# Attention and two mixtures of experts: a low part on GpSimd, an earlier gather, a reordered end

## The chip, the cores and the metric

The kernel runs on one core of a Trainium2 chip. The metric is device time in microseconds (us) of one execution, as the median of several. Before the change it is 914.06 us, the median of three runs (911.19 to 917.10). Each of the core's engines has its own instruction queue and runs it in order: TensorE (PE; PEld is its loading of weights), VectorE (DVE), ScalarE (ACT), GpSimd (POOL) and SyncE (SP), which here only issues DMAs.

## What is computed

Causal attention without a projection, then two mixtures of experts of which each token takes one expert. Cut to what matters (4 batches, 12 heads, 448 positions, 64 per head; 1792 tokens of 768, 8 experts, 1024 hidden):

```python
scores = scale * q @ k.T                  # masked above the diagonal
attn = exp(scores - max) / (sum + 1e-9)
x = attn @ v                              # heads side by side: 1792 x 768
# layer one: expert = argmax(normalized x . normalized embedding / tau)
# layer two: expert = argmax(x @ w_gate + modality_bias[modality_id])
for e in range(8):
    mask = expert_idx == e
    h = maximum(x[mask] @ w1[e], 0)
    out[mask] = gate_w[mask] * (h @ w2[e])
```

## The kernel before

Products that need more than one pass of precision are made from a high and a low half of each factor: `ah`, `al` are the halves of the attention weights `ex`, `w2h`, `w2l` those of a weight matrix, `hh`, `hl` those of the hidden layer, `xh`, `xl` those of the tokens.

**Attention** goes over 24 pairs of heads (two heads `e` = 0, 1 at a time). One loop, with `g` from 0 to 26, holds four stages of four different pairs: scores and exponentials of pair `g`, turned and split weights of pair `t = g - 1`, products with the values of pair `v = g - 2`, and a piece of the routing of layer one for pair `r = g - 3`. The code order is the order of every engine's queue. The weights of pair `g` leave the exponential as `ex`. `halves_hi` (L428), at the end of iteration `g`, makes `ah` (f16) of head 0 on ScalarE (L432) and of head 1 on GpSimd (L434), and has SyncE turn each with a transposing DMA (L425) into `th`. `halves_lo` (L436), one iteration later, makes `al = ex * ASC - ah` of both heads on VectorE (L439), and SyncE turns each into `tl`. In between VectorE makes `pl` (L455), the low part of those blocks that TensorE turns itself (L449). Two iterations after its exponentials, `values` (L484) multiplies `th`, `tl`, `ph`, `pl` with the halves of the values, and `combine` (L495 to L503) scales the result with `rinv` into `xb`.

On SyncE an iteration issues the loads for a later pair (L375, L381), the two `tl` of pair `g - 1`, at most times a store of finished tokens (L533), and the two `th` of pair `g`. On GpSimd it scales the queries of a later pair (L385), makes `ah` of head 1, and splits values (L163).

The routing of layer one is a generator; `tick()` takes a step of it after certain instructions on VectorE, so that its small steps stand between those of attention. When a batch of 448 tokens has its experts, GpSimd scatters its rows of `meta` (L653), a table of which token goes to which place.

**Each layer of experts** runs in blocks of 128 tokens. `gather_early` (L765 to L743) takes a block's rows of `meta` into `mg` and its tokens into `xg`; the first one stands in iteration 24 (`g == NPR`). TensorE turns them (L957) and multiplies (L975 to L977: `w1h xh`, `w1l xh`, `w1h xl`). The second layer has no routing inside, and works with up to `MAXB` = 21 blocks; here 17 are run, sections `j` up to 16. Section `j` computes the hidden layer of block `j` and the `down` product of block `j - 1` (L1040). `h_split` makes `hh` and `hl`, `x_squares` turns the tokens of block `j + 2` on VectorE into `xr` (L948). `split_w(2, ...)` makes the eight parts of `w2h` (ACT, L707) and `w2l` (VectorE, L709) of an expert from `w2r`, which was loaded long before. After the last section the last block's product runs in `down_last` (L1057), in two halves of 384 columns; if the expert changes at the last block (`cl > 0`, as here), `split_w(2)` stands ahead of it. Each half is scaled (L1070) into `yb` or `yT` and scattered to the output by GpSimd (L1071).

Of the kernel before, what the change touches and what calls it, by code (L numbers as in the profile page):

```python
# [35 lines left out]
ALIGN = 1  # L36
SPREAD = 4
# [19 lines left out]
def attention_two_moe_kernel(  # L57
# [370 lines left out]
    def halves_hi(g):  # L428
        for e in range(2):
            ah, ex = ahs[g % NAH][:, e, :, :CP], exs[g % NEX][:, e, :ND]  # L430
            if e == 0:
                act.activation(ah, ex, AF.Copy, scale=ASC)  # L432
            else:
                pool.tensor_scalar(out=ah, in0=ex, scalar1=ASC, scalar2=1.0, op0=ALU.mult, op1=ALU.mult)  # L434
            transposed(ths[g % NTH], ahs[g % NAH], e)

    def halves_lo(g, es):
        for e in es:
            vec.scalar_tensor_tensor(out=als[g % NAH][:, e, :, :CP], in0=exs[g % NEX][:, e, :ND], scalar=ASC,  # L439
                                     in1=ahs[g % NAH][:, e, :, :CP], op0=ALU.mult, op1=ALU.subtract)  # L440
            transposed(tls[g % NTH], als[g % NAH], e)
            tick()
# [351 lines left out]
    for g in range(NPR + 3):  # L794
# [28 lines left out]
        if 0 <= t < NPR:  # L823
            halves_lo(t, (0,))
        next(parts[0], None)
        if 0 <= t < NPR:
            halves_lo(t, (1,))
# [55 lines left out]
        if g + 1 < NPR:  # L883
            split_v(g + 1)
        if LEAD <= g <= NPR:
            for c in range(g - LEAD, KD if g == NPR else g - LEAD + 1):
                load_lead(m1, 1, c)
# [8 lines left out]
        if g == NPR:  # L896
# [5 lines left out]
            m1.gather_early((0,), 2 * S)  # L902
# [154 lines left out]
    def down_last(m, mg):  # L1057

        ops = ps_a.tile([P, 2, 512], F32, tag="av", name="o")
# [4 lines left out]
        for n in range(2):  # L1064
            cols = slice(n * 384, (n + 1) * 384)
            for f in range(KF):
                for w, h, st in ((w2h, hh, 0), (w2l, hh, 1), (w2h, hl, 2)):
                    pe.matmul(ops[:, n, :384], lhsT=h[f // KH][:, f % KH], rhs=w[f][:, cols],
                              start=(f == 0 and st == 0), stop=(f == KF - 1 and st == 2))
            act.activation(yhs[n], ops[:, n, :384], AF.Copy, scale=mg[:, 2:3])  # L1070
# [232 lines left out]
    def switches(m, tab):  # L1303
# [17 lines left out]
        vec.tensor_mul(chg, chg, actv[0:1])  # L1321
        vec.tensor_reduce(out=chg[:, 0:1], in_=chg[:, :MAXB], axis=AX.X, op=ALU.add)
# [17 lines left out]
    def run(m, is_full):  # L1340
# [8 lines left out]

        def section(j):  # L1350
# [10 lines left out]
            near = m.routed and j >= NBLK - 1  # L1361
            if 1 < j and j + 2 < MAXB:
                m.gather_q(j + 2)
            if near and j < NBLK:
                early_x(j)
# [4 lines left out]
            if FIRSTQ <= j + 1 < MAXB:  # L1370
                prep(m, j + 1, ra, MAXB if near and j >= NBLK else FIRSTQ + 1)
            if near and j >= NBLK:
# [28 lines left out]
            elif j > 1:  # L1401
                down(m, m.mg(j - 1), h_split)
# [30 lines left out]
        if not follow:  # L1433
            with tc.If(cl > 0) as other:  # L1434
                split_w(2)
# [102 lines left out]
```

## Time and profile before

| | |
|---|---|
| median of three runs | 914.06 us (911.19 to 917.10) |
| the profiled run | 911.23 us |
| its span in the trace | 909.4 us (1.8 us lie around it) |
| TensorE busy | 854.2 us (94%) |
| loading of weights | 738.0 us (81%) |
| VectorE busy | 681.7 us (75%) |
| ScalarE, GpSimd busy | 421.7 us (46%), 411.2 us (45%) |

The profile comes from one execution. A busy share is a mean over stretches with different limits, so each stretch has to be read by itself. A timeline row gives the start, the duration, engine, line, operation and what it writes and reads; a bracket at its end is the time for which the engine stood idle before, and what ended that. The rows of SyncE (SPq) are the time in which it issues a DMA; the DMA lands later.

### The profile page before, as it was taken

To read this page: it belongs to the slowest core of one execution; us is meant where nothing else is said; L and a number is where in the kernel's file an instruction comes from. 1 tells how busy PE (TensorE), PEld (TensorE's weight loads), DVE (VectorE), ACT (ScalarE), POOL (GpSimd) and SP (SyncE) were. 2 spreads that over 40 slices of the span, in tenths; PEclk is the share of its full clock that TensorE was granted. 3 is DMA by queue.
4 is the path that set the end of the run, shared out by engine and by line. 5 is a ranking of instruction groups with operands and counts; after the bars stand their busy time and mean duration, and the time that the engine had idled before them with its cause. 6 is when DMAs were issued, how large, how long until landed. Compare 5 with 4: busy or idle time off the path is not lost. (4 is left out here: it accounts for less than half of the span.)

```text
span 909.4 us, 20926 instructions
## 1 busy us (share of the span) xinstructions
PE 854.2 (94%) x6914; PEld 738.0 (81%) x6914; DVE 681.7 (75%) x1810; ACT 421.7 (46%) x777; POOL 411.2 (45%) x457
## 2 busy tenths in 40 slices
PE   5899999998598899999999999999999999999994
PEld 2577877777476799998898999988899898898984
DVE  5698999998694766788846874468886678976793
ACT  3576867776345564566524742254112133312323
POOL 4243345353345355454434564441653544544531
PEclk9899999999899999999999999999999999999998
DMA  6478776898617775588515563120281223511110
GB/s 200 104 144 149 174 158 149 173 161 184 223 28 241 270 289 188 189 278 300 206 38 176 188 227 121 39 90 6 58 332 39 66 86 134 186 48 54 54 38 16
DMA packets 92950, 131.94 MB, mean 145 GB/s; under 512 B 56877, under 2 KB 61283, under 8 KB 92784
## 3 DMA queue, kind: packets, MB, share of 16 engines
q1 hardware_dynamic: 79872, 103.25, 39.7%
q0 software_dynamic: 12912, 26.83, 9.5%
q8 instruction: 60, 0.98, 0.5%
q14 instruction: 106, 0.87, 0.3%
HBM read 101.48 MB, written 19.92 MB: 133 GB/s over the span
## 5 line engine op out<-in xcount | busy, mean ns | idle before, releaser
L759 POOL DMA_INDIRECT xg<-x,xi x128 | 137.2, 1072 | 102.4 <-DMA x<-yb,mg 55.0
L975 PE MATMUL h<-w1h,xh 128*128 128x512 f32 x408 | 164.2, 403 | 1.0 <-ACT xh L959 1.0
L976 PE MATMUL h<-w1l,xh 128*128 128x512 f32 x408 | 161.1, 395 | 0.8 <-DVE w1l L709 0.8
L977 PE MATMUL h<-w1h,xl 128*128 128x512 f32 x408 | 160.7, 394 | 0.0
L1040 PE MATMUL o<-w2h,hh 128*128 128x384 f32 x528 | 137.6, 341 | 0.2 <-ACT hh L989 0.2
L1040 PE MATMUL o<-w2h,hl 128*128 128x384 f32 x528 | 135.3, 337 | 0.9 <-DVE hl L990 0.9
L1040 PE MATMUL o<-w2l,hh 128*128 128x384 f32 x528 | 134.6, 336 | 0.0
L1017 DVE STREAM_TRANSPOSE hs<-h 32x256 f32<-32x256 f32 x240 | 107.1, 446 | 14.5 <-PE h L977 8.5
L422 ACT ACTIVATE ex<-sc,nm 112x112 f32<-112x112 f32 (+1 forms) x192 | 85.4, 496 | 48.8 <-DVE nm L417 47.9
L1040 PEld LDWEIGHTS o<-w2h,hl 128*128 128x128 f32 x528 | 95.3, 188 | 1.3 <-DVE hl L990 1.3
L1040 PEld LDWEIGHTS o<-w2l,hh 128*128 128x128 f32 x528 | 95.2, 188 | 0.4 <-DVE w2l L709 0.3
L1040 PEld LDWEIGHTS o<-w2h,hh 128*128 128x128 f32 x528 | 94.0, 188 | 1.8 <-ACT hh L989 0.4
L976 PEld LDWEIGHTS h<-w1l,xh 128*128 128x128 f32 x408 | 77.1, 189 | 18.2 <-DVE w1l L709 3.2
L1023 ACT ACTIVATE hh<-hs 128x512 fp32r<-128x512 f32 x30 | 18.4, 630 | 158.2 <-DVE hs L1017 79.6
L977 PEld LDWEIGHTS h<-w1h,xl 128*128 128x128 f32 x408 | 76.9, 189 | 17.7 <-DVE xl L960 0.3
L975 PEld LDWEIGHTS h<-w1h,xh 128*128 128x128 f32 x408 | 77.1, 189 | 16.6 <-ACT xh L959 1.1
L709 DVE TENSOR_TENSOR w1l<-w1r,w1h 128x1024 fp32r<-128x1024 f32 x66 | 76.4, 1220 | 9.2 <-ACT w1h L707 8.4
L417 DVE TENSOR_REDUCE nm<-sc 112x1 f32<-112x112 f32 (+1 forms) x192 | 74.6, 438 | 6.0 <-PE sc L411 5.9
L709 DVE TENSOR_TENSOR w2l<-w2r,w2h 128x768 fp32r<-128x768 f32 x78 | 68.7, 952 | 7.4 <-ACT w2h L707 6.6
L707 ACT CAST w1h<-w1r 128x1024 fp32r<-128x1024 f32 x64 | 62.4, 1047 | 9.3 <-PE h L977 5.2
L411 PE MATMUL sc<-r 64*112 64x112 f32 (+3 forms) x384 | 62.4, 447 | 3.9 <-DVE rt_ren L175 3.9
L948 DVE STREAM_TRANSPOSE xr<-xg 128x768 f32<-128x768 f32 x31 | 50.4, 1626 | 19.2 <-DMA xg<-x,xi 14.4
(327 smaller groups left out, 1776.9 us busy)
## 6 DMA issues: line engine op xcount, KB each, us to landing
w1r<-in_w1a SPq DMA_DIRECT2D x48, 512.0 KB, 6.2
w2r<-in_w2a SPq DMA_DIRECT2D x64, 384.0 KB, 6.4
r<-in_kqP SPq DMA_DIRECT2D x24, 448.0 KB, 4.5
w1r<-in_w1b SPq DMA_DIRECT2D x18, 512.0 KB, 5.7
w2r<-in_w2b SPq DMA_DIRECT2D x24, 384.0 KB, 6.5
vr<-in_vh SPq DMA_DIRECT2D x24, 224.0 KB, 4.3
x<-xb SPq DMA_DIRECT2D x16, 336.0 KB, 3.8
xg<-x,xi POOLq DMA_INDIRECT x128
```

The lines of the kernel that those rows point to most:

```text
L411: pe.matmul(scs[2 * g + e, c][:CP, :n], lhsT=r[rs, 1, c * CP : n], rhs=r[rs, 0, :n], start=False, stop=True, skip_group_check=True)
L417: vec.tensor_reduce(out=nms[h][:, c : c + 1], in_=scs[h, c][:CP, : CP * (c + 1)], axis=AX.X, op=ALU.min)
L422: act.activation(dst, scs.pop((h, c))[:CP, :n], AF.Exp, bias=nms[h][:, c : c + 1], scale=-1.0)
L707: act.copy(hi[k], r[k])
L709: vec.tensor_sub(lo[k], r[k], hi[k].bitcast(F32))
L759: pool.indirect_dma_start(out=xgs[j % 3][:, q * (D // Q) : (q + 1) * (D // Q)], out_offset=None, in_=quarters, in_offset=IND(ap=xi[:, q : ...
L948: vec.transpose(xr.rearrange("p k (q r) -> p q k r", q=Q), xgs[j % 3].rearrange("p (q r k) -> p q k r", q=Q, k=KD))
L975: pe.matmul(hps, lhsT=xh[:, c], rhs=w1h[c][:, ns], start=(c == 0), stop=False)
L976: pe.matmul(hps, lhsT=xh[:, c], rhs=w1l[c][:, ns], start=False, stop=False)
L977: pe.matmul(hps, lhsT=xl[:, c], rhs=w1h[c][:, ns], start=False, stop=(c == KD - 1))
L1017: vec.transpose(hr[cols, :, rows], hps[rows, q * 256 : (q + 1) * 256].rearrange("p (c k) -> p k c", c=QR))
L1040: pe.matmul(ops[:, n, :384], lhsT=h[f // KH][:, f % KH], rhs=w[f][:, n * 384 : (n + 1) * 384], start=(f == 0 and st == 0), stop=(f == KF - ...
```

## The change

Three edits.

*Attention.* The low part of head 1 moves from VectorE to GpSimd. GpSimd now scales `ex` of head 1 in place, copies it to `ah` and subtracts; this stands in `halves_hi`, at the end of iteration `g`. `halves_lo` keeps head 0 alone, with one `tick()` instead of two.

*First gather of layer one.* `gather_early((0,), ...)` stands at the end of iteration 22 instead of 24.

*End of layer two.* In sections from `j = 13` on, three parts of `w2` (`SOON`) are split ahead of `h_split` when this block is the last and its expert differs (`split_last`, a load and a branch on ACT and VectorE), and `x_squares` moves behind that. Ahead of `down_last` only five parts are left. `down_last` puts its halves into two PSUM tiles, and each half is scaled by ACT and VectorE together, 192 columns each.

```diff
--- before.py
+++ after.py
@@ -34,6 +34,7 @@
 ASC = 32768.0
 TICKS = 6
 ALIGN = 1
+SOON = 3
 SPREAD = 4
 LATE = 12
 LEAD = 18
@@ -431,15 +432,17 @@
             if e == 0:
                 act.activation(ah, ex, AF.Copy, scale=ASC)
             else:
-                pool.tensor_scalar(out=ah, in0=ex, scalar1=ASC, scalar2=1.0, op0=ALU.mult, op1=ALU.mult)
+                pool.tensor_scalar(out=ex, in0=ex, scalar1=ASC, scalar2=1.0, op0=ALU.mult, op1=ALU.mult)
+                pool.tensor_scalar(out=ah, in0=ex, scalar1=1.0, scalar2=1.0, op0=ALU.mult, op1=ALU.mult)
             transposed(ths[g % NTH], ahs[g % NAH], e)
-
-    def halves_lo(g, es):
-        for e in es:
-            vec.scalar_tensor_tensor(out=als[g % NAH][:, e, :, :CP], in0=exs[g % NEX][:, e, :ND], scalar=ASC,
-                                     in1=ahs[g % NAH][:, e, :, :CP], op0=ALU.mult, op1=ALU.subtract)
-            transposed(tls[g % NTH], als[g % NAH], e)
-            tick()
+        pool.tensor_tensor(out=als[g % NAH][:, 1, :, :CP], in0=ex, in1=ah, op=ALU.subtract)
+        transposed(tls[g % NTH], als[g % NAH], 1)
+
+    def halves_lo(g):
+        vec.scalar_tensor_tensor(out=als[g % NAH][:, 0, :, :CP], in0=exs[g % NEX][:, 0, :ND], scalar=ASC,
+                                 in1=ahs[g % NAH][:, 0, :, :CP], op0=ALU.mult, op1=ALU.subtract)
+        transposed(tls[g % NTH], als[g % NAH], 0)
+        tick()
 
     def turned_part(g, part):
 
@@ -821,10 +824,8 @@
         if g < NPR:
             both(expo, g, 1, ticks=False)
         if 0 <= t < NPR:
-            halves_lo(t, (0,))
+            halves_lo(t)
         next(parts[0], None)
-        if 0 <= t < NPR:
-            halves_lo(t, (1,))
         if g == NPR + 2:
             warm(ps_T, "T", WV)
         if 0 <= r < NPR:
@@ -882,6 +883,8 @@
             split_v(0)
         if g + 1 < NPR:
             split_v(g + 1)
+        if g == NPR - 2:
+            m1.gather_early((0,), 2 * S)
         if LEAD <= g <= NPR:
             for c in range(g - LEAD, KD if g == NPR else g - LEAD + 1):
                 load_lead(m1, 1, c)
@@ -899,7 +902,6 @@
             wb = left("wb", 1)
             w1l = [wb.tile([P, F], F32R, name=f"w1l{c}") for c in range(KD)]
             w2r = [wb.tile([P, D], F32, name=f"w2r{f}") for f in range(KF)]
-            m1.gather_early((0,), 2 * S)
             load_lead(m1, 2)
         if g == NPR + 2:
             split_w(1, (), range(3, KD))
@@ -1056,7 +1058,7 @@
 
     def down_last(m, mg):
 
-        ops = ps_a.tile([P, 2, 512], F32, tag="av", name="o")
+        ops = (o_tile()[:, 0], ps_h.tile([P, 512], F32, tag="h", name="o1"))
         yhs = yb[:, :384], yT.rearrange("p k c -> p (k c)")[:, :384]
         for n in range(2):
             vec.tensor_scalar(out=two[n], in0=mg[:, 1:2].bitcast(I32), scalar1=2.0, scalar2=float(n), op0=ALU.mult,
@@ -1065,9 +1067,10 @@
             cols = slice(n * 384, (n + 1) * 384)
             for f in range(KF):
                 for w, h, st in ((w2h, hh, 0), (w2l, hh, 1), (w2h, hl, 2)):
-                    pe.matmul(ops[:, n, :384], lhsT=h[f // KH][:, f % KH], rhs=w[f][:, cols],
+                    pe.matmul(ops[n][:, :384], lhsT=h[f // KH][:, f % KH], rhs=w[f][:, cols],
                               start=(f == 0 and st == 0), stop=(f == KF - 1 and st == 2))
-            act.activation(yhs[n], ops[:, n, :384], AF.Copy, scale=mg[:, 2:3])
+            act.activation(yhs[n][:, :192], ops[n][:, :192], AF.Copy, scale=mg[:, 2:3])
+            vec.tensor_scalar_mul(yhs[n][:, 192:], ops[n][:, 192:384], mg[:, 2:3])
             i = pool.indirect_dma_start(out=out.rearrange("n (k d) -> (n k) d", k=2), out_offset=IND(ap=two[n], axis=0),
                                         in_=yhs[n], in_offset=None, bounds_check=2 * NT - 1, oob_is_err=False)
             apart(i.ins, "out")
@@ -1319,6 +1322,8 @@
         if m.routed:
             vec.tensor_tensor(out=tab[:, 1, 1:], in0=chg[:, 1:], in1=actv[0:1, :MAXB], op=ALU.add)
         vec.tensor_mul(chg, chg, actv[0:1])
+        if not m.routed:
+            vec.tensor_copy(tab[:, 1, 1:], chg[:, 1:])
         vec.tensor_reduce(out=chg[:, 0:1], in_=chg[:, :MAXB], axis=AX.X, op=ALU.add)
         vec.tensor_copy(tab[:, 1, 0:1], chg[:, 0:1])
 
@@ -1347,6 +1352,10 @@
             with tc.If(ends < j + 2):
                 follow.gather_early((0, 1), what="x")
 
+        def split_last(j):
+            with tc.If(nc.values_load(tab[0:1, 1, j : j + 1], engines=[ENG.Activation, ENG.DVE], min_val=0, max_val=1) > 0):
+                split_w(2, range(SOON), range(SOON))
+
         def section(j):
 
             late = j >= LATE
@@ -1358,18 +1367,19 @@
                 split_next(m, j - 1, 2, tab)
             begin = m.routed and j != 2
             finish = m.routed and j not in (1, 3)
-            near = m.routed and j >= NBLK - 1
+            near = j >= NBLK - 1
+            ahead = MAXB if m.routed and j >= NBLK else FIRSTQ + 1
             if 1 < j and j + 2 < MAXB:
                 m.gather_q(j + 2)
-            if near and j < NBLK:
+            if m.routed and j == NBLK - 1:
                 early_x(j)
             if j + 4 < MAXB:
                 m.gather_m(j + 4)
                 m.gather_r(j + 4)
             ra, rb = (route_a(), chain(route_g(), route_b())) if finish else (iter(()), iter(()))
             if FIRSTQ <= j + 1 < MAXB:
-                prep(m, j + 1, ra, MAXB if near and j >= NBLK else FIRSTQ + 1)
-            if near and j >= NBLK:
+                prep(m, j + 1, ra, ahead)
+            if m.routed and j >= NBLK:
                 early_x(j)
             h0 = up(j, 0)
             if begin:
@@ -1399,7 +1409,9 @@
             if j > 1 and m.routed:
                 down(m, m.mg(j - 1), h_turned, {4: h_turn})
             elif j > 1:
-                down(m, m.mg(j - 1), h_split)
+                down(m, m.mg(j - 1), lambda: (split_last(j) if near else None, h_split()))
+                if near and j + 2 < MAXB:
+                    x_squares(j + 2)
             else:
                 if m.routed:
                     h_turn()
@@ -1432,7 +1444,7 @@
                 section(j)
         if not follow:
             with tc.If(cl > 0) as other:
-                split_w(2)
+                split_w(2, range(SOON, KF), range(SOON, KF))
                 down_last(m, gt)
             with other.Else():
                 down_last(m, gt)
```

How this moves instructions, in three places. First SyncE's queue in the middle of attention; `r` and `vr` are the loads for later pairs, `x` is the store of tokens, `x2` means both heads. Before:

```order
L375 DMA r_2442<-in_kqP 128x896
L381 DMA vr_2444<-in_vh 112x512
L425 DMA_TRANSPOSE tl_226<-al_220 128x4x112 x2
L533 DMA x_62<-xb_484 112x768
L425 DMA_TRANSPOSE th_221<-ah_217 128x4x112 x2
L375 DMA r_2643<-in_kqP 128x896
```

And of the change:

```order
L376 DMA r_2456<-in_kqP 128x896
L382 DMA vr_2458<-in_vh 112x512
L426 DMA_TRANSPOSE tl_226<-al_220 128x4x112
L536 DMA x_62<-xb_488 112x768
L426 DMA_TRANSPOSE th_221<-ah_217 128x4x112 x2
L426 DMA_TRANSPOSE tl_224<-al_219 128x4x112
L376 DMA r_2658<-in_kqP 128x896
```

The second transpose of the `tl` has moved from behind the loads to behind the two `th` of its own pair; the first `tl` of a pair follows behind the next loads, and so after it.

Second GpSimd's queue in iterations 22 and 23; `r...<-vr` and the row below it split values, `ld_full` is a flag that says whether the block is full. Before, iteration 23 into what follows it:

```order
L163 TENSOR_TENSOR r_242<-vr_4133 112x8x64
L163 TENSOR_TENSOR r_4783<-r_242 112x512
L434 TENSOR_SCALAR ah_218<-ex_216 112x4x112
L160 TENSOR_SCALAR w1h_5027<-w1r_329 128x1024
L160 TENSOR_SCALAR w1h_5028<-w1r_330 128x1024
L652 MEMSET pad 128x1
L653 DMA meta_63<-mt_138,r1sir_5115 14336x8
```

...and after four such scatters the gathers, with the root of the last batch's routing behind them:

```order
L653 DMA meta_63<-mt_138,r1sir_5115 14336x8
L765 TENSOR_LOAD ld_fullm_199
L765 ISA x2
L767 COMPARE_AND_BRANCH
L740 DMA mg_323<-meta_63,ld_idxm_197 128x8
...
L743 DMA xg_322<-x_62,mg_323 128x768
...
L170 TENSOR_TENSOR rt_sr_5422<-r1ss_5273,half 112x4
```

And of the change:

```order
L438 TENSOR_TENSOR al_219<-ex_215,ah_217 112x4x112
L164 TENSOR_TENSOR r_242<-vr_4140 112x8x64
L164 TENSOR_TENSOR r_4808<-r_242 112x512
L768 TENSOR_LOAD ld_fullm_199
...
L743 DMA mg_323<-meta_63,ld_idxm_197 128x8
...
L746 DMA xg_322<-x_62,mg_323 128x768
...
L435 TENSOR_SCALAR ex_216<-ex_216 112x448
L436 TENSOR_SCALAR ah_218<-ex_216 112x4x112
L438 TENSOR_TENSOR al_220<-ex_216,ah_218 112x4x112
L161 TENSOR_SCALAR w1h_5052<-w1r_329 128x1024
```

The gathers have moved from behind the third batch's scatters to ahead of the three instructions that make head 1's halves of the last pair; those three are one before.

Third VectorE's queue at the end of section 16 of layer two, the last that runs here; `hs` are the turned hidden values, `gt` a copy of the block's rows of `meta`. Before:

```order
L1017 STREAM_TRANSPOSE hs<-h 32x8x32 x8
L948 STREAM_TRANSPOSE xr<-xg_322 128x4x6x32
L1024 SCALAR_TENSOR_TENSOR hl_5490<-hs,hh_5492 128x512
L1024 SCALAR_TENSOR_TENSOR hl_5491<-hs,hh_5493 128x512
L1410 COPY gt<-mg_327 128x8
L1422 COMPARE_AND_BRANCH
```

And of the change:

```order
L1019 STREAM_TRANSPOSE hs<-h 32x8x32 x8
L1356 TENSOR_LOAD t_tabm_317
L1356 COMPARE_AND_BRANCH
L712 TENSOR_TENSOR w2l_5519<-w2r_5230,w2h_5521 128x768
L712 TENSOR_TENSOR w2l_5520<-w2r_5231,w2h_5522 128x768
L712 TENSOR_TENSOR w2l_5489<-w2r_5232,w2h_5523 128x768
L1356 UNCONDITIONAL_BRANCH x2
L1026 SCALAR_TENSOR_TENSOR hl_5514<-hs,hh_5516 128x512
L1026 SCALAR_TENSOR_TENSOR hl_5515<-hs,hh_5517 128x512
L950 STREAM_TRANSPOSE xr<-xg_322 128x4x6x32
L1422 COPY gt<-mg_327 128x8
L1434 COMPARE_AND_BRANCH
```

Three parts of `w2l` and a branch stand ahead of `hl`, and `xr` has moved from ahead of `hl` to behind it.

## Rows read from the trace of the kernel before

**Rows 1.** Windows of two pairs: length, busy us (count) per engine, TensorE's clock, DMA

```profile
99.06:107.14 8.08, 8.08 (x145) 6.43 (x145) 7.43 (x21) 6.43 (x15) 3.15 (x5) 1.00 0.88 198
126.35:136.11 9.76, 8.75 (x148) 6.74 (x148) 9.70 (x32) 5.70 (x13) 3.14 (x4) 1.00 0.63 132
```

**Rows 2.** Waits of TensorE, 40 to 232 us: total us, times, longest

```profile
PE av L484 <- DMA tl<-al: 2.9, 6, 0.7
PE tb L449 <- DVE pl L455: 2.6, 5, 0.8
PE tb L512 <- DVE xb L503: 1.5, 3, 0.6
```

**Rows 3.** Timeline of one smooth pair, GpSimd, VectorE and TensorE: start, duration, what

```profile
104.30 0.56 POOL L434 TENSOR_SCALAR ah<-ex 112x448 f16<-112x448 f32 x1 [4.85 <-ACT ex L422]
...
106.95 0.56 POOL L385 TENSOR_SCALAR r<-r 128x448 f32<-128x448 f32 x1
...
105.70 0.17 DVE L495 TENSOR_SCALAR rinv<-av 112x8 f32<-112x8 f32 x1 [0.39 <-PE tb L488]
...
107.83 0.61 DVE L439 SCALAR_TENSOR_TENSOR al<-ex,ah 112x448 f16<-112x448 f32 x1
108.37 0.61 DVE L455 SCALAR_TENSOR_TENSOR pl<-tb,ph 112x448 f16<-112x448 f32 x1
108.90 0.61 DVE L439 SCALAR_TENSOR_TENSOR al<-ex,ah 112x448 f16<-112x448 f32 x1
...
109.04 0.30 PE L449 MATMUL tb<-ident,ex 112*112 112x112 f32 x1
```

**Rows 4.** Groups of VectorE and GpSimd, 40 to 232 us: busy us, mean ns, idle before

```profile
L439 DVE SCALAR_TENSOR_TENSOR al<-ex,ah 112x448 f16<-112x448 f32 x44 | 27.5, 625 | 0.0
...
L163 POOL TENSOR_TENSOR r<-r 112x512 bf16<-112x512 f32 x21 | 21.8, 1040 | 1.6
```

**Rows 5.** Timeline: VectorE beside GpSimd's subtractions, at the first pair and in routing

```profile
19.16 1.04 POOL L163 TENSOR_TENSOR r<-vr 112x512 f32<-112x512 f32 x1
...
19.91 0.76 DVE L439 SCALAR_TENSOR_TENSOR al<-ex,ah 112x448 f16<-112x448 f32 x1
...
182.75 1.03 DVE L606 SCALAR_TENSOR_TENSOR r1lgr<-r1lgr,tau_r,r1nrr 112x32 f32<-112x32 f32 x1
```

**Rows 6.** Tile tl: time to landing; timeline of SyncE and TensorE for one pair

```profile
DMA to landing us min/median/max: 3.1/4.4/5.8
...
110.84 2.50 SPq L425 DMA_TRANSPOSE tl<-al  x2
...
115.98 0.19 PE L484 MATMUL av<-vr,tl 112*128 112x64 bf16 x1
...
117.27 0.20 PE L484 MATMUL av<-vr,tl 112*128 112x64 bf16 x1 [0.65 <-DMA tl<-al]
```

**Rows 7.** Timeline of GpSimd, VectorE and TensorE where layer one begins

```profile
230.91 1.06 POOL L653 DMA_INDIRECT meta<-mt,r1sir  x1 [10.52 <-DVE ld_rowm L286]
...
241.02 1.66 POOL L740 DMA_INDIRECT mg<-meta,ld_idxm  x1 [4.93 <-DMA meta<-mt,r1sir]
...
247.33 0.17 DVE L175 TENSOR_SCALAR rt_rr<-rt_sr 112x4 f32<-112x4 f32 x1 [3.25 <-POOL rt_sr L170]
...
249.21 1.54 PE L957 MATMUL xt<-ident,xg 128*128 128x128 f32 x6 [6.51 <-DMA xg<-x,mg]
...
251.77 0.63 PE L977 MATMUL h<-w1h,xl 128*128 128x512 f32 x1
```

**Rows 8.** Timeline of VectorE, TensorE and ScalarE at the end of layer two

```profile
883.53 1.62 DVE L948 STREAM_TRANSPOSE xr<-xg 128x768 f32<-128x768 f32 x1
...
888.41 7.04 DVE L709 TENSOR_TENSOR w2l<-w2r,w2h 128x768 fp32r<-128x768 f32 x8 [1.57 <-ACT w2h L707]
...
896.84 0.44 PE L1068 MATMUL o<-w2h,hh 128*128 128x384 f32 x1 [0.72 <-ACT yb L1070]
...
901.35 0.58 ACT L1070 ACTIVATE yT<-o,gt 128x384 f32<-128x384 f32 x1 [4.56 <-PE o L1068]
```

## The prediction

> **What bounds the kernel now.** I read the windows first, then who waits for whom at TensorE, then each place that the change touches as a timeline. Attention runs to about 240 us, the first mixture of experts to about 600 us, the second to 909 us. The change touches attention and the two ends of the mixtures.
>
> In attention the windows [rows 1] show two kinds of head pair. In a smooth one (99.06 to 107.14) TensorE is busy throughout and VectorE for 7.43 of 8.08 us. In a crowded one (126.35 to 136.11), into which the routing of a finished batch is woven, VectorE is busy for 9.70 of 9.76 us and TensorE for 8.75: there VectorE sets the pace. What TensorE waited for over all pairs is short [rows 2]: 2.9 us for the transposed low part `tl`, 2.6 us for `pl`, 1.5 us for `xb`. By these waits part one can win 7.0 us at most.
>
> A busy TensorE does not mean that VectorE has room. Follow one smooth pair [rows 3]: VectorE starts `rinv` at 105.70 after waiting 0.39 us for TensorE, and `pl` ends 3.28 us later, at 108.98, with `al` of head 0 (107.83) just ahead of it. TensorE's next transposes (L449) start at 109.04, 0.06 us after `pl`. So the loop goes from `rinv` to `pl` on VectorE and from there back to the next `rinv` on TensorE, and has no slack. `al` of head 0 lies in that loop. `al` of head 1, which the change takes away, starts at 108.90, behind `pl`, in the part where VectorE later waits for TensorE.
>
> **Part one: the low part of head 1 moves to GpSimd.** VectorE loses one `al` per pair, 625 ns busy [rows 4], of which 0.53 us is pitch (108.37 to 108.90 in rows 3). GpSimd gains a scaling in place of 112x448 (a scaling, L385, takes 0.56 us [rows 3]) and a subtraction: its 112x512 subtraction takes 1040 ns [rows 4], so 448/512 of that is 0.91 us. Together 1.5 us per pair. GpSimd idled 4.85 us ahead of its `ah` [rows 3], so it has the time.
>
> The Trainium skill ("GPSIMD Engine Reference", 4.1 Engine selection) advises against this: it gives elementwise work to VectorE and calls GpSimd about 2 times slower with two inputs. By that factor the subtraction would take 1.25 us and still fit into the idle time; the rows here give 0.91 against 0.625, a factor near 1.5.
>
> What it saves: in smooth pairs nothing, since the removed `al` is not in the loop. In the crowded ones up to 0.53 us each: TensorE's eight waits for `pl` and `xb` total 4.1 us [rows 2], and eight times 0.53 is as much. I take half, **-2.0 us** (0 to -4.1), as many of those waits begin ahead of the removed instruction.
>
> What it costs on VectorE: GpSimd's later work slides by 1.5 us. In a smooth pair it now ends at 107.51 (106.95 + 0.56), just ahead of head 0's `al` at 107.83 [rows 3]; afterwards it runs to about 109.0 and covers that `al`. How far that hurts is seen at the first pair, where `al` ran under GpSimd's subtractions: 0.76 us [rows 5] instead of 0.61. So 0.15 us per pair, in the loop; with some 20 pairs and part of it absorbed I take **+2.0 us** (0 to +3). A worse row exists: L606 on VectorE, only 112x32, took 1.03 us [rows 5], the length of the GpSimd subtraction that it ran beside. That is a rival below.
>
> The Trainium skill ("GPSIMD Engine Reference", 1. Specifications) says that GpSimd shares its SBUF interfaces with VectorE and contends with instructions there that have two SBUF inputs; `al` is one, and the 0.76 us agrees. It gives no price.
>
> What it does to SyncE's queue: two transposing DMAs hold SyncE for 2.50 us [rows 6], so 1.25 us each. Now both `tl` go out behind the loads of an iteration. Afterwards `tl` of head 1 goes out directly behind the two `th`, some 2.5 us earlier, and `tl` of head 0 stays behind the loads and goes out 1.25 us later. Landing takes 3.1 to 5.8 us, median 4.4 [rows 6]. In the pair whose two went out from 110.84 TensorE first used `tl` (head 0) at 115.98, then waited 0.65 us for head 1 until 117.27 [rows 6]. Head 0 had 115.98 - 110.84 - 4.4 = 0.74 us of room; 1.25 us later it is half a microsecond late. So the six waits for head 1 (2.9 us) go, and shorter ones for head 0 come in more pairs. A wait in one pair gives a later one its time back, so I count 0.2 us in each of 20 pairs, 4 us. Net **+1.0 us** (-2.9, no pair late, to +9.5, half of 1.25 us in every pair).
>
> Part one together: +1.0 us, between -7.0 and +9.6 without the rival's hold on VectorE.
>
> **Part two: the first gather moves from pair 24 to pair 22.** TensorE waited 6.51 us for `xg`, until 249.21 [rows 7]. GpSimd's queue was the cause: the gather of `mg` stood at 241.02, after 4.93 us for the last `meta`; the gather of `xg` had to wait for it, and `rt_sr`, the root of the last batch's routing, stood behind both. Afterwards `xg` has landed some 20 us ahead of its use. On GpSimd the two gathers then stand ahead of pair 23's `ah` and hold it for some 5 us (two issues and a landing); TensorE is two pairs, 16 us, behind that `ah`, which covers it. Without the cover it would cost those 5 us.
>
> What is late next is VectorE. `rt_sr` now stands directly behind the four scatters of `meta`, which began at 230.91. With one call fewer per pair the routing generator finishes the third batch later, behind pair 23's combine; I put the scatters at 238.5 to 243.3, so `rt_sr` ends at 244.4. VectorE is through `w1l` at 245.3 (now at 244.08, which is 247.33 less the wait of 3.25). Then come its short chain and a flag's load, 1.9 us (now from 247.33 to TensorE's start at 249.21), and half of `xl`, about 0.6: 247.8 us. TensorE's first L977, which waits for that `xl`, stood at 251.77 [rows 7]. That is 4 us; as the scatters may slip by more I take **-3.5 us** (-2 to -6.5, the whole wait).
>
> **Part three: the end.** VectorE waited 1.57 us for ACT's first cast, then made eight `w2l` from 888.41 to 895.45, 0.87 us apart; TensorE followed and ended the first half at 896.12, waited 0.72 us for `yb` and ended the second at 901.35, and `yT` took 0.58 us [rows 8]. Afterwards three parts are split ahead of `hl`. ACT's casts for them have time, since it only waits for VectorE's `hs` there. VectorE's order becomes three `w2l`, two `hl`, `xr` (1.62 us, now ahead of `hl`), five `w2l`. From 883.53 that is 2.7 + 0.5 for a branch + 1.3 + 1.6 + 0.8 for a copy and branches + 4.4 = 11.3, so 894.8. Only 0.65 us are won, not the 2.6 us of three parts, since the wait of 1.57 us is all that there is to fill. The wait of 0.72 us goes, as each half has its own PSUM tile. The eviction in two pieces on two engines saves about 0.2 of 0.58 us, by its length. Together 1.57, so **-1.5 us** (-0.5, if TensorE and not VectorE is late, to -2.2). The load and branch in the near sections and the moved `xr` cost nothing: `hl` is wanted only one section of TensorE's work later.
>
> **Sum.** +1.0 - 3.5 - 1.5 = -4.0 us on the profiled run's 911.23 us gives 907.2 us. The median of the three runs is 914.06, so the same step from there is **910 us**.
>
> **The rivals.** *Relief without the cost*: `al` is not slowed, the crowded pairs win the full 4.1 us, head 0's `tl` lands in time in most pairs (-1.5). With parts two and three -10.6: 903.5 us. For it: 9.70 of 9.76 us on VectorE in a crowded pair. Against: the loop of rows 3.
> *GpSimd holds VectorE* (the other side): head 0's `al` is held until the subtraction over it ends, near 108.5, as L606 was: 0.7 us in each of 20 pairs. -2 + 14 + 1 - 5 = +8: 922 us. For it: L606. Against: the same instruction lost only 0.15 us at 19.91. The kernel gets slower than before once `al` is held by over 0.3 us per pair.
> *Head 0's `tl` late in every pair*: -2 + 2 + 9.5 - 5 = +4.5: 918.6 us. For it: 0.74 us of room against 1.25. Against: a landing of 3.1 us is still in time.
> *The early gather wins nothing*, as the last batch's routing is as late as before: 1.0 - 1.5 = -0.5: 913.6 us. Against: `rt_sr` now waits behind `xg`.
>
> **How the numbers follow.** About 1% (9 us) is what a measurement of this kernel can tell from no change. Forecast 0.50, relief 0.18, gather without gain 0.12, GpSimd holding 0.10, `tl` late 0.10. Faster by over 1% needs under 904.9 us: most of relief and a little of the forecast, 0.20. Slower by over 1% needs over 923.2 us: a part of the two late cases, 0.08. The rest, 0.72, is within 1%. The range of 901 to 919 leaves out the better end of relief and the worse ends of the late cases; the forecast's own range is 905 to 915.
>
> **What would show it.** `pl` of a smooth pair ends later than 3.28 us after `rinv`, or not; `al` reads 0.6, 0.76 or over 1.2 us; TensorE's waits for `tl` move from head 1 to head 0; the crowded pairs get shorter than 9.7 us; L957 and L977 start some 4 us sooner; the second half of the end begins without a wait. The prediction is wrong if smooth pairs shorten, or if L977 starts where it did.

## The result and the profile after

The changed kernel takes 923.35 us (median of four runs), the kernel before 913.68 us beside it (four runs, 911.19 to 917.10): a ratio of 1.0101, 95% interval 1.0059 to 1.0142. Three of the four runs of the changed kernel lie between 922.63 and 923.60 us; the fourth, a slow one of 3396.37 us, is left out of the ratio. The forecast was 910 us with a range of 901 to 919. The time came out slower than before, 4.35 us above the range, and close to the 922 us of the rival "GpSimd holds VectorE".

The profiled run took 923.09 us with a span of 921.3 us, against 911.23 and 909.4. The difference of 11.9 us in the span builds up like this (events of after minus the same events of before):

| place | later than before by |
|---|---|
| `pl` of pair 4 / 10 / 16 | 0.37 / 4.42 / 6.99 us |
| `pl` of pair 22 / 23 | 14.36 / 12.08 us |
| first product with `xl` (L977, now L979) | 7.10 us |
| first to fourth `down` product of layer one | 8.67, 8.91, 10.44, 11.33 us |
| start of layer two's blocks | 12.56 us |
| last matmul / end | 11.58 / 11.88 us |

So attention lost some 12 us, the start of layer one won back 5, the first blocks of layer one lost 4 of these again, and the end won 1.0 us up to the last matmul and lost 0.3 behind it.

The lines of the changed kernel have moved by a few: `al` is L442, `pl` L458, the turned blocks L452, GpSimd's `ex`, `ah`, `al` L435, L436, L438, its splits L164 and its scaling L386. First the waits of TensorE from 40 to 240 us (total, times, longest), beside [rows 2]:

```profile
PE tb L452 <- DVE pl L458: 12.9, 17, 1.5
PE av L487 <- DMA tl<-al: 5.0, 5, 2.5
PE tb L515 <- DVE xb L506: 1.5, 3, 0.6
```

The wait for `pl` has grown from 2.6 to 12.9 us, 17 times instead of 5. Where it comes from is seen in a smooth pair (timeline: start, duration, engine; beside [rows 3]):

```profile
107.93 0.57 POOL L435 TENSOR_SCALAR ex<-ex 112x448 f32<-112x448 f32 x1 [3.50 <-ACT ex L423]
108.58 0.57 POOL L436 TENSOR_SCALAR ah<-ex 112x448 f16<-112x448 f32 x1
109.23 1.04 POOL L438 TENSOR_TENSOR al<-ex,ah 112x448 f16<-112x448 f32 x1
109.33 0.17 DVE L498 TENSOR_SCALAR rinv<-av 112x8 f32<-112x8 f32 x1 [0.39 <-PE tb L491]
111.35 1.04 POOL L164 TENSOR_TENSOR r<-r 112x512 bf16<-112x512 f32 x1
111.47 1.40 DVE L442 SCALAR_TENSOR_TENSOR al<-ex,ah 112x448 f16<-112x448 f32 x1
112.36 0.94 POOL L386 TENSOR_SCALAR r<-r 128x448 f32<-128x448 f32 x1
112.79 0.61 DVE L458 SCALAR_TENSOR_TENSOR pl<-tb,ph 112x448 f16<-112x448 f32 x1
113.46 0.59 PE L452 MATMUL tb<-ident,ex 112*112 112x112 f32 x4 [0.62 <-DVE pl L458]
```

GpSimd's last split starts at 111.35, VectorE's `al` 0.12 us after it. `al` takes 1.40 us instead of 0.61 and ends at 112.87, 0.48 us after the split has ended (112.39). `pl` now ends at 113.40, 4.07 us after the start of `rinv` instead of 3.28: the 0.79 us by which `al` is longer is all of it, and TensorE waits for it. GpSimd is held in turn: its scaling of the queries takes 0.94 us instead of 0.56, as it starts while `al` still runs. Over all pairs (tile `al`, beside [rows 4]):

```profile
L442 DVE SCALAR_TENSOR_TENSOR al<-ex,ah x22: 608/1399/1471, 41.3 to 234.7; 112x448 f16<-112x448 f32 x22
L438 POOL TENSOR_TENSOR al<-ex,ah x21: 1034/1038/1045, 47.2 to 236.9; 112x448 f16<-112x448 f32 x21
```

The median of `al` is 1399 ns, and all its 24 calls (two stand ahead of 40 us) are longer than 0.61 us by 13.1 us together. Of the 24, 18 take over 0.65 us, and each of these ends 0.48 us after the GpSimd instruction that ran when it started. A smooth pair takes 8.87 us instead of 8.08 (windows, beside [rows 1]: length, busy us and count of PE, PEld, DVE, ACT, POOL, clock, DMA):

```profile
104.59:113.46 8.87, 8.24 (x145) 6.47 (x145) 7.68 (x19) 6.43 (x15) 5.12 (x6) 1.00 0.64 163
```

At the start of layer one (beside [rows 7]) the wait of 6.51 us for `xg` is gone:

```profile
250.09 1.03 POOL L656 DMA_INDIRECT meta<-mt,r1sir  x1 [10.10 <-DVE ld_rowm L287]
255.06 1.21 POOL L171 TENSOR_TENSOR rt_sr<-r1ss,half 112x4 f32<-112x4 f32 x1
255.34 1.57 PE L959 MATMUL xt<-ident,xg 128*128 128x128 f32 x6
258.87 0.80 PE L979 MATMUL h<-w1h,xl 128*128 128x512 f32 x1 [0.74 <-DVE xl L962]
```

The order is as forecast: scatters, then `rt_sr`, then VectorE's chain and `xl`. The end (beside [rows 8]):

```profile
900.90 1.53 DVE L950 STREAM_TRANSPOSE xr<-xg 128x768 f32<-128x768 f32 x1
902.35 0.12 DVE L1422 COPY gt<-mg 128x8 f32<-128x8 f32 x1
902.59 0.44 PE L1070 MATMUL o<-w2l,hh 128*128 128x384 f32 x1 [2.51 <-DVEq L1434]
902.71 3.77 ACT L710 CAST w2h<-w2r 128x768 fp32r<-128x768 f32 x5 [3.17 <-DVEq L1434]
903.58 4.43 DVE L712 TENSOR_TENSOR w2l<-w2r,w2h 128x768 fp32r<-128x768 f32 x5 [1.10 <-ACT w2h L710]
912.93 0.42 ACT L1072 ACTIVATE yT<-o,gt 128x192 f32<-128x192 f32 x1 [3.73 <-PE o L1070]
913.38 0.42 DVE L1073 TENSOR_SCALAR yT<-o,gt 128x192 f32<-128x192 f32 x1 [3.74 <-ACT yT L1072]
```

All engines meet at the branch (L1434) behind VectorE's `gt`, which now stands behind `xr`. So ACT's five casts start only at 902.71, and VectorE waits 1.10 us for the first: the wait of 1.57 us that was to be filled is for the most part still there, one branch later. The two pieces of the eviction run one after the other, 0.87 us from 912.93 to 913.80, where one piece took 0.58.

### The profile page after: what moved, and what is told of

It is laid out like the page before. It is cut to its first block, busy times and chain, and to the rows that moved or that the text cites. A ratio compares the mean times of both kernels' runs of the same rounds, so it can differ in the third digit from the quotient of the medians.

```text
span 921.3 us, 20978 instructions
## 1 busy us (share of the span) xinstructions
PE 859.2 (93%) x6914; PEld 742.2 (81%) x6914; DVE 684.2 (74%) x1789; ACT 421.3 (46%) x777; POOL 450.7 (49%) x505
## 5 line engine op out<-in xcount | busy, mean ns | idle before, releaser
L977 PE MATMUL h<-w1h,xh 128*128 128x512 f32 x408 | 164.8, 404 | 1.0 <-ACT xh L961 1.0
L979 PE MATMUL h<-w1h,xl 128*128 128x512 f32 x408 | 161.6, 396 | 0.7 <-DVE xl L962 0.7
L979 PEld LDWEIGHTS h<-w1h,xl 128*128 128x128 f32 x408 | 77.2, 189 | 19.2 <-DVE xl L962 1.8
L977 PEld LDWEIGHTS h<-w1h,xh 128*128 128x128 f32 x408 | 77.4, 190 | 16.6 <-ACT xh L961 1.1
```

The costliest lines, as they stand in the source:

```text
L977: pe.matmul(hps, lhsT=xh[:, c], rhs=w1h[c][:, ns], start=(c == 0), stop=False)
L979: pe.matmul(hps, lhsT=xl[:, c], rhs=w1h[c][:, ns], start=False, stop=(c == KD - 1))
```

## The experiments

Ratios are to runs of the kernel before on the same chip, with 95% intervals. One profile differs from another by some us where the program is the same: `e4_parts23` and `e11_oneact` below are one program up to the last evictions, and at L977 the second is 3.1 us ahead, at the fourth `down` product 1.4 us behind. So what a trace says of a place is taken from the place, and of the whole time from the ratio.

**The parts apart.** `e1_part1` has the edits to `halves_hi` and `halves_lo` alone, `e2_part2` the moved `gather_early` alone, `e3_part3` the edits at the end alone, `e4_parts23` both of the latter; each is a subset of the diff above.

> Part one alone (the low part of head 1 on GpSimd). Theory 'hold': a GpSimd instruction that is running keeps VectorE's al of head 0 until it ends; al reads about 1.4 us in most pairs and its excess over 0.61 us, some 13 us in all, is the loss: +11 to +14 us against the kernel before. Theory 'late tl': the loss comes from head 0's tl, so TensorE's waits for tl rise by more than those for pl. If attention's loss were mostly made by the early gather, this run would be near +5.

> Part two alone (first gather at pair 22). Theory 'kept': L977 starts about 4 us sooner and the end comes 3 to 4 us sooner. Theory 'given back': the first blocks of layer one wait for other data of the last batch's routing, so that the end is within 1.5 us of the time before though L977 starts sooner. In this run the generator has its two calls per pair as before, so the scatters are not late and the gain at L977 may reach 5 us.

> Part three alone (the end of layer two). From the changed kernel's trace: between the last down product and TensorE's last matmul about 1.0 us less, and the two-piece eviction one behind the other (0.87 instead of 0.58 us) gives 0.3 back: -0.5 to -1 us, not to be told from no change. My step in the prediction said -1.5.

> Parts two and three without part one. If the parts add: the sum of the two runs before, -1 to -5 us, so 909 to 913. If it is near the changed kernel's time instead, part one is not the cause.

| kernel | ratio | `pl` of pair 23 | L977 |
|---|---|---|---|
| `e1_part1` | 1.0132 (1.0056 to 1.0208) | +13.52 us | +10.39 us |
| `e2_part2` | 0.9996 (0.9969 to 1.0022) | +1.84 us | -1.53 us |
| `e3_part3` | 1.0012 (0.9982 to 1.0041) | +0.68 us | +0.41 us |
| `e4_parts23` | 0.9963 (0.9931 to 0.9995) | +0.63 us | -3.32 us |

(The last two columns are the profile's times less those of before.) Part one alone makes the kernel slower by about 12 us, as theory 'hold' said; its `al` has a median of 1.33 us. Part two wins 3.4 us between pair 23 and L977 (from +1.84 to -1.53), as forecast at that place; in `e4_parts23` it is 4.0 us. Alone neither it nor part three can be told from no change, so the 3 to 4 us that theory 'kept' expected of part two at the end aren't seen; together they win 0.4%, within what was expected.

**Is it the hold?** `e5_cover` leaves attention as before, and gives GpSimd two more instructions per pair on scratch tiles, so that only its time beside VectorE changes (the scratch tiles' lines are cut):

```diff
+                pool.tensor_scalar(out=scr, in0=scr, scalar1=1.0, scalar2=1.0, op0=ALU.mult, op1=ALU.mult)
                 pool.tensor_scalar(out=ah, in0=ex, scalar1=ASC, scalar2=1.0, op0=ALU.mult, op1=ALU.mult)
+                pool.tensor_tensor(out=scr16, in0=scr, in1=ah, op=ALU.subtract)
```

> The kernel before, and on GpSimd per pair one more scaling of 112x448 and one more subtraction of 112x448, both on scratch tiles (head 1's ah included as input); VectorE keeps both al, SyncE's queue is untouched, and nothing reads the scratch. Theory 'hold': VectorE's al is held as in the changed kernel, the first of the two al of a pair reads about 1.4 us, and the time rises by 10 to 18 us (VectorE also keeps the second al). Theory 'late tl': nothing is later on SyncE, so within 2 us of before.

It is slower: 1.0081 (1.0051 to 1.0111). No work of VectorE was added or removed, and `pl` of pair 23 stands 9.92 us later. The rows of a pair (timeline, GpSimd and VectorE's two `al`):

```profile
109.51 1.04 POOL L163 TENSOR_TENSOR r<-r 112x512 bf16<-112x512 f32 x1
110.19 0.84 DVE L444 SCALAR_TENSOR_TENSOR al<-ex,ah 112x448 f16<-112x448 f32 x1
110.52 0.94 POOL L388 TENSOR_SCALAR r<-r 128x448 f32<-128x448 f32 x1
111.43 0.55 POOL L437 TENSOR_SCALAR scr<-scr 112x448 f32<-112x448 f32 x1
111.49 0.97 DVE L444 SCALAR_TENSOR_TENSOR al<-ex,ah 112x448 f16<-112x448 f32 x1
```

The first `al` ends at 111.03, 0.48 us after the split (110.55), the second at 112.46, 0.48 us after the scaling (111.98). The second shows that a GpSimd instruction with one input holds `al` as one with two does. All 48 calls are longer than 0.61 us by 8.06 us together, which is near the rise of the time (7.4 us by the ratio, 8.7 us by the medians). TensorE waits 8.4 us for `pl` and 0.3 us for `tl` in attention, so the loss comes by way of `al` and not of the transposes. The expectation was right on the hold and too high in size: `al` takes 0.84 and 0.97 us here instead of 1.4, since less of GpSimd's instruction is left when it comes, and the loss is below the 10 to 18 us.

**Is it the place of `tl`?** `e6_tlorder` is part one with `tl` of head 1 issued where it was, behind the loads of the next iteration:

```diff
         pool.tensor_tensor(out=als[g % NAH][:, 1, :, :CP], in0=ex, in1=ah, op=ALU.subtract)
-        transposed(tls[g % NTH], als[g % NAH], 1)
...
         transposed(tls[g % NTH], als[g % NAH], 0)
+        transposed(tls[g % NTH], als[g % NAH], 1)
```

> Part one alone, but the transposing DMA of head 1's tl is issued behind that of head 0 again, at its old place in SyncE's queue. Theory 'hold': as part one alone, +11 to +14 us, al near 1.4 us. Theory 'late tl': the loss is gone or below 4 us. In between, the difference to part one alone is the share of tl.

It came out between the two theories, at 1.0047: `al` is held as in the changed kernel (median 1.38 us), and part of the loss is gone with the old order.

**Without the hold.** `e7_swap` is part one with the heads exchanged: GpSimd makes both halves of head 0, and VectorE's remaining `al` is that of head 1, behind `pl`, where GpSimd is done by then. `e8_swap23` is the same in the whole changed kernel. Against part one, cut to two of its places:

```diff
-        pool.tensor_tensor(out=als[g % NAH][:, 1, :, :CP], in0=ex, in1=ah, op=ALU.subtract)
+        pool.tensor_tensor(out=als[g % NAH][:, 0, :, :CP], in0=ex[0], in1=ah[0], op=ALU.subtract)
...
-        if 0 <= t < NPR:
-            halves_lo(t)
         next(parts[0], None)
+        if 0 <= t < NPR:
+            halves_lo(t)
```

> Part one with the heads exchanged: GpSimd makes both halves of head 0, ScalarE the high and VectorE the low half of head 1, and that al stands behind pl, outside the loop. GpSimd does as much as in part one. Theory 'hold': pl no longer waits for a held al; a smooth pair gets up to 0.17 us shorter (ph is there at 108.20, pl starts at 108.37), the crowded pairs up to 0.5 us, tl of head 0 is early: -3 to -8 us against before, even if al still reads over 0.61 us. A theory by which GpSimd's added work as such slows VectorE, wherever al stands, expects a loss of over 5 us.

> The changed kernel with the heads exchanged as in the run before (parts two and three unchanged): the run before and about -3 us for the two other parts, so -6 to -11 us, 905 to 910. By the other theory a loss.

Both expected a gain and both were slower than before, by 0.42% and 0.47%: the hold is gone, and something else still costs.

**Neither.** `e9_swaptl` exchanges the heads and issues both `tl` behind the loads as before; `e10_swaptl23` adds parts two and three. Against `e7_swap`, cut; the same line is gone from behind the `th`:

```diff
     def halves_lo(g):
+        transposed(tls[g % NTH], als[g % NAH], 0)
         vec.scalar_tensor_tensor(out=als[g % NAH][:, 1, :, :CP], in0=exs[g % NEX][:, 1, :ND], scalar=ASC,
```

> Part one alone with the heads exchanged (GpSimd makes both halves of head 0, VectorE the low part of head 1 behind pl), and both tl issued behind the loads of an iteration, as in the kernel before, instead of tl of head 0 directly behind the th. The exchanged version alone stood at 1.0042 of before, though al was no longer held; its smooth pairs took 8.05 us, but around 190 us single waits of TensorE for tl of 2.6 us stood in pairs in which loads of the first expert's weights share SyncE's queue. Theory (what is left of the cost is the place of the tl in SyncE's queue): no tl wait above 1.0 us, pl of pair 23 within 1.5 us of before (the exchanged version: 3.5 later), al again 0.62 us, and the time between 0.997 and 1.002 of before. Rival (what is left lies in GpSimd's longer work, which makes ah and so th of head 0 late, or behind attention): pl of pair 23 again some 3 us later, TensorE waits for th instead of tl, and the time stays between 1.003 and 1.006.

> The same with parts two and three of the change. Theory: what parts two and three gave without part one (0.9963 of before) comes on top of a part one that costs nothing: 0.993 to 0.999, about 909 to 914 us, and at the first product with xl (L977) 2 to 4 us ahead of before. Rival: part one keeps a cost, and the time lies between 1.000 and 1.005.

The time of `e9_swaptl` is as its theory said, but one wait for `tl` of 1.6 us is left (1.0 was expected at most), and `pl` of pair 23 stands 3.4 us ahead of before. `e10_swaptl23` hits neither range: 0.9997, with L977 0.8 us ahead in its trace, whose run took 919.21 us, the longest of twelve.

The six kernels that hold part one, by what they keep of its two costs:

| | second `tl` directly behind `th` | both `tl` behind the loads |
|---|---|---|
| `al` held, part one alone | `e1_part1` 1.0132 (1.0056 to 1.0208) | `e6_tlorder` 1.0047 (1.0018 to 1.0076) |
| `al` free, part one alone | `e7_swap` 1.0042 (1.0010 to 1.0075) | `e9_swaptl` 0.9990 (0.9972 to 1.0008) |
| `al` free, with parts two and three | `e8_swap23` 1.0047 (1.0015 to 1.0079) | `e10_swaptl23` 0.9997 (0.9977 to 1.0017) |

The changed kernel itself is the missing corner (held, directly behind `th`, with parts two and three): 1.0101.

Down a column, the hold costs 0.9% in the first (where the interval is wide) and 0.57% in the second, about 5 us. The versions were run in different sets, each against before in its own set, and such a difference has an interval of some 3 us either way (where `e1_part1` is one of the two, some 8). The exchange takes the hold away: in `e9_swaptl` the tile `al` reads

```profile
L439 DVE SCALAR_TENSOR_TENSOR al<-ex,ah x22: 606/614/915, 44.0 to 220.3; 112x448 f16<-112x448 f32 x22
```

and in its smooth pair GpSimd's last instruction has started ahead of `pl`, and `al` runs behind it at 0.61 us:

```profile
107.95 0.56 POOL L385 TENSOR_SCALAR r<-r 128x448 f32<-128x448 f32 x1
107.95 0.62 DVE L455 SCALAR_TENSOR_TENSOR pl<-tb,ph 112x448 f16<-112x448 f32 x1 [0.38 <-ACT ph L453]
108.49 0.61 DVE L439 SCALAR_TENSOR_TENSOR al<-ex,ah 112x448 f16<-112x448 f32 x1
```

`pl`, which reads one of its inputs from PSUM, ran beside GpSimd at 0.62 us: it isn't held.

Along a row, the place of `tl` costs 0.9%, 0.52% and 0.50%: again about 5 us (the second and the third rest on the same two sets of before). In `e7_swap` smooth pairs take 8.05 us (before: 8.08), but around 190 us TensorE waits once for long (timeline of SyncE and TensorE):

```profile
183.46 0.39 SPq L696 DMA_DIRECT2D w1r<-in_w1a  x1
183.89 0.43 SPq L375 DMA_DIRECT2D r<-in_kqP  x1
184.42 0.37 SPq L381 DMA_DIRECT2D vr<-in_vh  x1
184.89 1.23 SPq L425 DMA_TRANSPOSE tl<-al  x1
186.22 2.57 SPq L425 DMA_TRANSPOSE th<-ah  x2
188.88 1.67 SPq L425 DMA_TRANSPOSE tl<-al  x1
190.95 0.20 PE L484 MATMUL av<-vr,tl 112*128 112x64 bf16 x1 [2.47 <-DMA tl<-al]
```

Here three loads, one `tl`, two `th` and the next pair's `tl` stand in one queue. The changed kernel has the same wait, 2.55 us until 196.94; with both `tl` in their old place the longest is 0.8 (`e6_tlorder`), 1.6 (`e9_swaptl`) and 2.2 us (`e10_swaptl23`), in the same stretch. So the old order shortens that wait and doesn't remove it. All waits for `tl` from 40 to 238 us together differ between the two orders by 1.4 to 2.3 us (`e7_swap` 3.3 and `e9_swaptl` 1.9, `e8_swap23` 4.7 and `e10_swaptl23` 3.1, `e1_part1` 3.1 and `e6_tlorder` 0.8), which is less than the 5. That the order costs time is shown; by what way it costs the rest, the traces don't show plainly, and it stays open.

**A version that beats both.** `e11_oneact` is parts two and three without part one, with the last evictions whole on ScalarE:

```diff
-            act.activation(yhs[n][:, :192], ops[n][:, :192], AF.Copy, scale=mg[:, 2:3])
-            vec.tensor_scalar_mul(yhs[n][:, 192:], ops[n][:, 192:384], mg[:, 2:3])
+            act.activation(yhs[n], ops[n][:, :384], AF.Copy, scale=mg[:, 2:3])
```

> Parts two and three without part one, and the last two evictions whole on ScalarE (384 columns in one instruction each) instead of 192 columns on ScalarE and 192 on VectorE; the two PSUM tiles stay. Theory (the two pieces of one tile ran one after the other, 0.87 us, where one piece took 0.58): the eviction takes about 0.58 us, the step from the last matmul to the end is 0.3 us shorter than in the change, and the time is that of parts two and three (0.9963 of before, 0.993 to 0.9995) or 0.0003 less, which the measurement can't tell. Rival (parts two and three gave nothing, and the 0.9963 was chance): 0.999 to 1.002.

It takes 909.16 us against 912.55, a ratio of 0.9959 (0.9934 to 0.9983); `e4_parts23` gave 0.9963 in another set of runs. The eviction takes 0.58 us again:

```profile
898.65 0.58 ACT L1072 ACTIVATE yT<-o,gt 128x384 f32<-128x384 f32 x1 [3.59 <-PE o L1070]
```

## Why the prediction was wrong, step by step

**The step that failed: "So 0.15 us per pair, in the loop", +2.0 us for the slowed `al`.** The loop of [rows 3] was right, and so was it that GpSimd's later work would come to lie over head 0's `al`. The price was misread. The row at 19.91 [rows 5] was taken for an `al` that ran beside GpSimd's subtraction and lost only 0.15 us. It didn't run beside it: the subtraction at 19.16 ended at 20.20, only 0.29 us after `al` had been counted as started, and `al` ended at 20.67, 0.47 us after it. That is the same 0.47 to 0.48 us as in the rows of after and of `e5_cover`, where more of GpSimd's instruction was left. So the row of before already showed a full hold, of an `al` that happened to arrive late. The row behind it, which the prediction did not look at, shows the other side (timeline of before):

```profile
20.27 1.30 POOL L163 TENSOR_TENSOR r<-r 112x512 bf16<-112x512 f32 x1
```

The same subtraction takes 1.04 us elsewhere; here GpSimd waited for `al`. A second full hold stands later in the same trace, under a scaling with one input; `al` ends at 177.71, again 0.47 us after it (177.24):

```profile
176.68 0.56 POOL L385 TENSOR_SCALAR r<-r 128x448 f32<-128x448 f32 x1
176.89 0.82 DVE L439 SCALAR_TENSOR_TENSOR al<-ex,ah 112x448 f16<-112x448 f32 x1
```

Duration is then not a price but a coincidence of starts: what counts is how much of the other engine's instruction is left. In the smooth pairs 0.92 us was left (from 111.47 to 112.39), and `al` cost 0.79 us more.

The rival "GpSimd holds VectorE" had the right mechanism and row (L606) and nearly the right price (0.7 us), and got 0.10. The argument against it was the misread row. That its 922 us came so close is in part luck: it let 14 us of hold through to the end, put 1 us on the place of `tl` and took 7 us off for relief and the two other parts. The comparisons below give about 5 us for the hold, about 5 for `tl` and nothing off.

The Trainium skill has the rule in "SBUF — State Buffer", section "SBUF: two separate sides": VectorE and GpSimd share a pair of ports under an exclusive lock, and against a VectorE instruction with two SBUF inputs whoever starts first has it for the whole instruction. The runs agree: 0.79 us of hold under a split of 1.04 us, 0.38 us for GpSimd's scaling in return, none for `pl`. The prediction drew on another page, which gives no price.

**The relief, -2.0 us.** It is there, but elsewhere than in the waits that were counted. `e9_swaptl`, without both costs, reaches `pl` of pair 23 3.38 us ahead of before and L977 7.8 us ahead. The last 4.4 us of that are part two's gain, won without part two: with one `tick()` fewer per pair the third batch's scatters come later in the program, so the first gather, still in iteration 24, already stands ahead of them on GpSimd (timeline of `e9_swaptl`, beside [rows 7]):

```profile
221.98 1.10 POOL L740 DMA_INDIRECT mg<-meta,ld_idxm  x1 [0.17 <-issue]
225.29 0.95 POOL L743 DMA_INDIRECT xg<-x,mg  x1 [2.21 <-DMA mg<-meta,ld_idxm]
235.20 0.95 POOL L653 DMA_INDIRECT meta<-mt,r1sir  x1 [8.84 <-DVE ld_rowm L286]
239.89 1.57 PE L955 MATMUL xt<-ident,xg 128*128 128x128 f32 x6
```

`e1_part1` shows the same order (`mg` at 237.81, the scatters from 253.39), and without part two it, `e6_tlorder` and `e7_swap` win 3.1, 5.9 and 3.9 us there. `e5_cover`, which keeps the two calls of `tick()`, shows no gain (+9.92 at pair 23, +9.73 at L977). The prediction saw that the scatters would slip, and used it for what is late next, but not that this alone removes the wait. So the -3.5 us counted for part two come with part one as well, and on top of part one parts two and three win nothing that can be measured (`e10_swaptl23` against `e9_swaptl`, 0.9997 and 0.9990).

**`tl` in SyncE's queue, +1.0 us.** The direction was right and the size wrong: about 5 us in three comparisons. The prediction looked at the room of head 0's `tl` in a smooth pair; the longest waits stand in pairs into which loads of the first expert's weights come as well, and they explain only a part.

**Part two, -3.5 us.** Right at its place (3.4 us in `e2_part2`). In some traces what is won up to L977 is partly given back in the first blocks of layer one: in `e9_swaptl` the lead shrinks from 7.8 us at L977 to 3.45 at the fourth `down` product, in the changed kernel the lag grows from 7.10 to 11.33. TensorE's wait at the counting product `pr` is 1.41 us in before, 3.08 in after and 3.88 in `e9_swaptl`, and VectorE's `xr` in front of it, which took its tokens without a wait in before, waits 1.56 and 2.41 us there. In that stretch the DMA engines are full (windows of after, columns as above):

```profile
300.00:310.00 10.00, 6.57 (x28) 4.50 (x28) 7.53 (x20) 2.41 (x5) 7.86 (x9) 0.96 1.01 364
310.00:320.00 10.00, 10.00 (x45) 9.75 (x46) 7.77 (x18) 6.71 (x8) 1.69 (x2) 0.69 0.71 270
```

The DMA share is 1.01 where TensorE is busy for 6.57 of 10 us, and behind the wait the granted clock is 0.69, a mean between the two levels of 1.2 and 2.4 GHz; before had 1.00 in all three stretches from 290 to 320 us. But this isn't the price of the early gather, and full DMA engines don't decide it: `e2_part2` and `e4_parts23` have the early gather and keep their lead (-1.53 to -2.05, -3.32 to -3.93 us), with waits of 1.38 and 1.45 us at `pr`, though the DMA share of `e4_parts23` is 1.01 from 290 to 300 us as well. `e11_oneact`, the same program as `e4_parts23` up to there, waits 2.95 us. What decides between the short and the long wait stays open.

**Part three, -1.5 us.** -1.0 us at the last matmul (0.4 to 1.0 in the traces of the kernels that have part three) and +0.3 behind it. The step of 0.5 us for the branch left out that all engines meet there behind `gt`, and so behind the moved `xr` of 1.53 us. The second half does start without a wait. The eviction in two pieces saves nothing: the two pieces of one tile ran one after the other.

**The sum.** By the comparisons the change is about +5 us for the hold, +5 us for the order of `tl`, and nothing for the rest: 10 us, against the 9.7 measured. Each of the two has an interval of some 3 us either way, and `e5_cover` puts the hold alone at 7.4, so the sum is rougher than it looks. Against the terms of the forecast:

| term | forecast | by the comparisons |
|---|---|---|
| slowed `al` | +2.0 us | about +5 us |
| place of `tl` | +1.0 us | about +5 us |
| relief, part two and part three | -7.0 us | -0.9 us without (`e9_swaptl`) and -0.3 us with (`e10_swaptl23`) parts two and three |

The misread row is the step whose mechanism was wrong, but the term furthest off is the last one. Its gains do stand at their places, and most of them don't reach the end: `e9_swaptl` leads by 7.8 us at L977 in its trace, and by 0.1% in the whole time. In the same set of runs parts two and three without part one stand at 0.9959 (`e11_oneact`, below 1 by its whole interval) and with the cheap form of part one at 0.9997 (`e10_swaptl23`), so part one still takes their gain away when neither of its two costs is left. Where it goes behind L977 is open.

One bound was also added up wrongly: the upper ends of part one, 0, +3 and +9.5, make +12.5 us and not +9.6. Part one alone measured about +12 us.

## What to carry to other kernels

When work is moved to GpSimd, draw which VectorE instructions with two SBUF inputs its later instructions will then lie over, and price each at the rest of GpSimd's instruction that is still to run, not at a duration found where the two happened to overlap little. Put the overlapped instruction behind one that reads PSUM, or outside the loop, before giving up the move. And when a generator is stepped by calls, count what a removed call does to the order of everything behind it: it may already do what another edit is meant to do.

## What the runs showed of the hardware

VectorE's 112x448 `al`, with two SBUF inputs, ends 0.47 to 0.48 us after the GpSimd instruction that ran when it came, whether that has one input (0.55 us) or two (1.04 us); this holds for all 18 `al` of over 0.65 us in after and all 26 in `e5_cover`. `pl`, with one input in PSUM, takes at most 0.63 us in every trace, though 17 of its 48 calls in after run beside GpSimd. GpSimd is held in turn: its next instruction takes longer when `al` still runs (0.94 instead of 0.56, 1.30 instead of 1.04). The hold is shown as duration, not as idle time: the waits of VectorE name nobody. GpSimd's subtraction of 112x448 to f16 took 1.04 us, as its 112x512 subtraction to bf16 does, so the forecast's 448/512 of that (0.91) was too low.
